# GateLoop attention and a PReLU MLP in one kernel: all steps in a new order

## The chip, the cores and the metric

The kernel runs on one core of a Trainium2 chip, and the metric is the device time of one execution in microseconds. A core has TensorE (PE, matmuls, with weight loads listed apart as PEld), VectorE (DVE), ScalarE (ACT), GpSimd (POOL) and SyncE (SP). Each runs its own instructions strictly in the order in which the program holds them; semaphores tie the engines together. Here SP does nothing but issue the 700 transfers.

## The reference

An attention block with complex gates (GateLoop) gives `attn_out`; its heads are joined and go through an MLP with a PReLU whose slope differs per feature.

```python
# q, k, v, a_re, a_im: (4, 8, 768, 48) float32
mag = np.sqrt(a_re * a_re + a_im * a_im)
scale = np.minimum(mag, 0.999) / (mag + 1e-06)
a_re_n, a_im_n = (a_re * scale, a_im * scale)
for t in range(S):
    ar, ai = (a_re_n[:, :, t, :, None], a_im_n[:, :, t, :, None])
    new_re = ar * S_re - ai * S_im
    new_im = ar * S_im + ai * S_re
    kv = np.einsum('bhd,bhe->bhde', k[:, :, t], v[:, :, t])
    S_re, S_im = (new_re + kv, new_im)
    y[:, :, t] = np.einsum('bhd,bhde->bhe', q[:, :, t], S_re)
x = attn_out.transpose(0, 2, 1, 3).reshape(B * S, H * D)   # 3072 x 384
h = x @ w_in                                               # w_in 384 x 2048
g = np.maximum(h, 0.0) + alpha * np.minimum(h, 0.0)
return (g @ w_out).astype(np.float32)                      # w_out 2048 x 384
```

## The kernel before

The recurrence is cut into 24 units (`unit`, from L563): 4 batch entries times 6 stretches of 128 tokens, with all 8 heads together. Inside a unit the tokens meet in six levels of doubling distance (1, 2, 4, 8, 16, 32, two levels per visit). For each level `meet` issues 16 small matmuls of keys with queries (L596) into `ps_lv`, ScalarE copies operands apart (WQ L660, W L676), VectorE multiplies queries and keys on by the decays (KQ L637) and masks the products (A L620, or ScalarE at L610). Then TensorE turns the keys (`ps_kt`, L708), multiplies them with the values (`ps_kv`, L720), VectorE carries the state `St` on (L728, L731), and TensorE sums the unit's result in `ps_y`: from the state (L746, 16 matmuls, two halves of 8) and from the masked products with the values VL (L760, 48 matmuls, in four steps of 12). ScalarE copies the result out (L771), SP writes it to DRAM (`ysc`).

Ahead of the units, nine tasks `gates` make decays (`decs`) and rotations (`phs`) of stretches of tokens out of `a_re` and `a_im`, mostly on VectorE and ScalarE; the results go through DRAM and come back as T and PP. `loads`, `half_rows` and `loads_v` issue the transfers of queries, keys, rotations, decays and values. `pieces` and two `weights` tasks load the MLP's weights as pairs of words and join them to f32 (L443, L445).

The MLP works on blocks of 256 tokens. `loads_x` loads a block as xT once both of its units have written their results. For the first two blocks `features` makes one feature row block at a time (TensorE L817, ScalarE L824, VectorE L826), and `outputs` sums over the features (L867). For the other ten, `two_features` makes two at a time (TensorE L839, ScalarE L848 and L852, VectorE L854), and `seven` takes the product with `w_out` apart into seven products of halves (L957, in `product`, folded by VectorE at L963 in `fold` or copied by ScalarE at L973). `all_mlp` is one task: the order inside the MLP is fixed, only what stands between its steps is not.

Every task is a Python generator that gives control back before each step; a step is one vector or scalar instruction, one transfer, or a group of matmuls. `Plan.run` goes through the string `ORDER` and advances the task of each letter by one step:

```python
    def run(self, order):
        for c in order:
            next(self.tasks[self.LETTERS.index(c)], None)
```

The letters are A to I for the nine `gates`, J `loads`, K `half_rows`, L `loads_v`, M `pieces`, N and O the two `weights`, P to Z and a to m the units 0 to 23, n `loads_x`, o `all_mlp`. Since a step issues its instruction at once, `ORDER` fixes the order of the instructions on all five engines and so also the order of the transfers in SP's queue, and with them which waits stand where. Buffers have fixed numbers of copies (three KQ, two T, one V and VL, one PP, two xT, two `ps_h`, two `ps_lv`, one each of `ps_y`, `ps_o`, `misc`), whatever the order is. The arguments of the steps (`PE(0.28, ..., n=16)`) have no effect in this program: `step` returns None.

Of the kernel before, what the change touches and what calls it, by code (L numbers as in the profile page):

```python
# [27 lines left out]


ORDER = (  # L30
    "ABMABAAABABAAAAAAABMAAAAAMAAAABABBBJMMNMAAAJABBAAKAAAKJJAAAAAAAABBBABJABBBBBBNMBNPBBBPNPJBJKJKJBJBBB"
    "PNBBBPBBBBBBBBBPPPOOOOJLJCPJJLLKKCPOJLLLMLLLLLLLMLLJJOPOPOPNOPPPPONNPPQCPPPQNQCCCCPPPPPPPPPPQQPQPCNC"
    "CCPPPPPPPPPCQQNCCCCCONCCCQOQCNPCPQQQOJMMJPPLMLLJCNQQNORCJLnLCMLLJJJLCCCLLLLQCQRCRQQCCOQNQQQoooooooLL"
    "LNQQRRQNooQQCCCCCNCooQoOoQRQoCQORCCNRRoNooooooORoQOMJONQQoooooRNNOOQQQQRQQROQOQDQQJLRLLnLJJORoLLoooo"
    "LLDMLRNNoLLLLLLooooJDooDDRoooSoSoRRRRRRRRooooooooDRRoRRoRooooRNNNRDSDoDRoDRDSOooooooooRoDoDRSSRJJJJR"
    "RSNSSRRRRDoooooDSDTOooODSLRRoSSoLMLLMJLJLLLLLooSoDSoOTSNoooooSNoOooSSoSoSNSSSSoSDooToSoSooSTSNoooOOo"
    "oNMLLLLLTTSoTSTDSOoTTSDoooooDoDSOKTNoNNNOSSSTSSTSJJJMJLSDDoooooSoooooDJLSSLoOToNTToooToOoOOoooooTTOT"
    "TToTDDTToooooUTnTTooLLLJJLJLDLLLUooooTDToDDoooLLLoLKDoJJJToTTUooDDoDDDTDJTDDDoooooUoTTUTUTTUUUUoVooo"
    "oooooUoTUUVUTTTTVooooooooUUUEJJLLLJJELLLLLLLLLJoLLooooVoEooooUUoUUUEoEVooooooEoEoUVUoUUUoooooUooooEU"
    "UVVUUVUVVVEEEooooooooVoUoKEUVKVUUUUJKKEUUUUKJJJVEVVooVooooEoooEEooEooVVVooooVVVVVVoWoWooooooVoVooJLL"  # L40
    "LJnWooVooVWoLLLLVWWEVEVEEEWEVWWLLLLLLLLEVWWVJEJoKJoooooooooooVVVWVWVVVELKVVLLLLJLJJLLLJJWoWWEWoooooo"
    "oooXXooEEEoEEoooooooooooooooooWWWWWWWoooWXoEWLLLoEoooooooooooWWooooWWoooXoXWWEEEWEEWoJLLLJoooWXWWWEW"
    "XWWWXYWXLWWLLFYXJLnLJJLoooooooXooooooooooooooXXXXXXoooooFoooooooXXFXXoXXXoXooooooooXoXoXYYooooLLLLLL"
    "LLooXXYYXooXYXYYLYooooXooooXFYFooooooXXXXYXYXFYoFYXXXLXLJLJJJLJLLLFooooooooYYoJooooooooooFoooooYYYFF"
    "YooYYooYYoJJLLLJLLJLoZoYooZooYooooFFoooFoYooYYFZoooFFLLooooooooooZooooZZYZYZYFZZYFYFYoooFZYYYZYZYYFo"
    "YooFFYooooooooooFFLLYJJJLooZooooooZZoooooooooooLnFLLFLJLLLJFooLJLLLLZaaFooooooZZoooZFaoFFZZoooooooaF"
    "FoZZZoZFFFoooooooZoooZooaaoooZoZoZZaaZFFFooFJJaoaaZooooooooooooZZZaZZZaZZaoooooooZaoaooabooooooooooo"
    "oooaaooabbZLLZLGJJLLJLJLLGLLLLLaaaoaaooaGooaoooooooJoboaoooaGoobGabaaaJJabbaLKKKoGbGoooooooooooobbbo"
    "ooGGooooGGooooboooooooooababaaGbaGGbGabaLaooooooooocoobLLJJGnKLoooooooooLoLLooobbooocbLLLLLJbbGGGoob"
    "ocooooooLLLKboboboooGGoboooocboooooobbccboocbGbGooooooocccGGoobboooobbbbooooooooooooGcGGKJGGGobcbcbo"  # L50
    "ocbJLJbbLLLJJLocccoooooooooooGooooccGcccocccGdGcoooooooooooocococoocooccoooGGGGcJLLLLLLLLLLdGcocGcoo"
    "oooooodoodooocccddcJJJcdcooooooooooooooooddLLccLHLcJJJLLLJLLdoLdHLLnoooooooodKLLLdddoddooooooooooooo"
    "ooddodddddooHeddoooeodooooodedoHdoooooooooooededdddeeoHddHooooooooeHeeoooHoooddoooooooooooooooddoeee"
    "oddoKJJJJddLLLJeJLLLJJJJLLLeoeoooooooooeHooooHooooooooooffHHooooeeeLJJLLLLLooooooHHHHHHHfooeeooeeeeo"
    "oooooeeoooooooooeoeoooeeeoeHHHfoHeHgefeoooooeeefeHeeKHooofofeeoJJHffoooooooonofHLJLLLLLLLHHooooooooo"
    "offfgoLLJLJJJLLLoofffooooooogHoLooooffoofHHfooooHHHoooooooooofffffoofoofoogoHooooHooooffooooofHHfffH"
    "ffHohhogooooooffgffgffofofhfgogooooooooooooooooggIJJLLLLLLLLJJJIJJgLLLLLLggIgoggIooooooIooooooooooog"
    "goghgIoggogoghIoogooooooogooIoogoogoghhgIhgghIhgoIooohhoooooooooioooooooohogIoIoghggghghhgIggLLLLJJn"
    "hhoooooooooooiLLLLLJLLLLLLJJooohhIhIhhIoooohhhIIihooooooooihoooooooooooooiIhooooooooooooooooooohhJoo"
    "oiiiihhohihIIIohihoooooooJhhihhihihLoohIIiooooooooooiihooooooooooooooiioihILLLoooIiiiijJJLLLJJLLLJji"  # L60
    "iJLLLLLIoiooiooiIiooioiIjiioIIIIIoIooooooooooIIIoiIoooooojiijijiijJIojjjjoooooooooooooooooooijjjjiio"
    "oiijJnJJJLLLLJLLojooooooooooooooooojjjjjjjkkjooooooooojjooojookooooooojoojoookookjkoooookkoooooooooo"
    "oojJJLLLLLLLLLjjoooooookoooooooooojookoooooookooojjjjkjkjjjkLjjkooooooooolkkoLLJJJJJooooookkkokkkook"
    "kooookokkooooolloookooklkllkkkkkloooollooooooooooolJLLLLLLLLLLJLLooooooooooloooooooooklkklkkkklkkLLL"
    "LLnlllooLLLJJLLooooooooooooooollolllloolllooooooolooolmmolloLLLLLoooooloooololmmlooooooooooolooooooo"
    "olmlmlmomomooooooooomoooooooooomoooolmlmlmooooomLLLLLLmomoooooooooLLLLoooooommoooommllmmmmmllLLLLooo"
    "oommoooooomooomooommmmmmmmmomooooooooooommmoooooooooooonoooooooooooooooooooooooooooooooooooooooooooo"
    "oooooooooooooooooooooooooooooooooooooooooooooooooooooooooooooooooooooooooooooooooooooooooooooooooooo"
    "oooooooooooooooooooooooooooooooooooooooooooooooooooooooooooooooooooooooooooooooooooooooooooooooo")

# [1072 lines left out]
```

## Time and profile before

| what | value |
|---|---|
| time of 3 runs, median (lowest to highest) | 764.36 us (761.99 to 765.21) |
| span of the profiled execution | 763.4 us |
| granted TensorE clock, mean | 0.998 |
| TensorE idle before its first matmul | 26.0 us |
| first matmul of the MLP | 84.4 us |
| last group of the last unit's product with VL (L760) | 688.8 us |
| DMA | 130.61 MB, mean 171 GB/s |

The profile is of one execution. Its page has the busy time of each engine, the span in 40 equal slices with a digit of busy tenths for each, the DMA queues, the chain of work that ended last and the costliest groups of instructions. Further views list instructions in order of time, merged where equal ones follow each other (start, time to the end of the last, engine, line, tiles and shapes, count), and busy times in stretches of the span. A matmul's time in these lists reaches from its start to the modelled end of its pipeline, so rows overlap; what TensorE really spends is read from start to start. An f32 matmul of the program stands as two passes in the trace (a transpose, L708, as one), so 16 matmuls of the program are 32 there.

Of the chain that ended last, 53% of the span lies on TensorE, 16% in transfers, 11% on VectorE and 4% on ScalarE. In the slices of VectorE and of the granted clock,

```profile
DVE  7889889998999799898986898888996765742323
PEclk9999999999999999999999999999999999999999
```

VectorE is busy through the first three quarters and TensorE's clock shows no tenth below 9.

### The profile page before, as it was taken

To read this page: it belongs to the slowest core of one execution; us is meant where nothing else is said; L and a number is where in the kernel's file an instruction comes from. 1 tells how busy PE (TensorE), PEld (TensorE's weight loads), DVE (VectorE), ACT (ScalarE), POOL (GpSimd) and SP (SyncE) were. 2 spreads that over 40 slices of the span, in tenths; PEclk is the share of its full clock that TensorE was granted. 3 is DMA by queue.
4 is the path that set the end of the run, shared out by engine and by line. 5 is a ranking of instruction groups with operands and counts; after the bars stand their busy time and mean duration, and the time that the engine had idled before them with its cause. 6 is when DMAs were issued, how large, how long until landed. Compare 5 with 4: busy or idle time off the path is not lost.

```text
span 763.4 us, 26774 instructions
## 1 busy us (share of the span) xinstructions
PE 674.9 (88%) x11728; PEld 581.2 (76%) x11728; DVE 605.4 (79%) x798; ACT 487.6 (64%) x886; POOL 13.1 (2%) x48
## 2 busy tenths in 40 slices
PE   0024578999999999999999999999999999999998
PEld 0024456776767888888888889888888988889987
DVE  7889889998999799898986898888996765742323
ACT  8868888985658576946693666756584544453330
POOL 5000000000000000000000000000000000000000
PEclk9999999999999999999999999999999999999999
DMA  9999989979677936787668854865745743421000
GB/s 257 273 258 230 267 236 274 232 216 245 192 194 201 254 83 140 210 223 187 177 170 210 234 123 102 227 188 135 185 129 171 183 104 81 112 43 53 1 21 21
DMA packets 177180, 130.61 MB, mean 171 GB/s; under 512 B 66280, under 2 KB 168424, under 8 KB 176616
## 3 DMA queue, kind: packets, MB, share of 16 engines
q1 hardware_dynamic: 177064, 128.91, 64.3%
q8 instruction: 92, 1.51, 0.9%
q14 instruction: 24, 0.20, 0.1%
HBM read 100.52 MB, written 35.42 MB: 178 GB/s over the span
## 4 chain that ended last, share of the span: by engine, by line
PE 53%; DMA 16%; DVE 11%; SPq 6%; ACT 4%; issue 2%; DVEq 0%; ACTq 0%
PE ps_h L839 19%; PE ps_o L957 17%; PE ps_lv L596 4%; PE ps_y L760 3%; DVE KQ L637 3%; DMA PP<-phs 3%; PE ps_o L867 3%; DMA T<-decs 2%; PE ps_kv L720 2%; SPq L547 2%; PE ps_y L746 2%; DMA xT<-ysc 2%; DMA shared<-in_w_out_dram 2%; DMA VL<-vsc 2%; PE ps_h L817 1%
## 5 line engine op out<-in xcount | busy, mean ns | idle before, releaser
L839 PE MATMUL ps_h<-xT,w_in_sb 128*128 128x256 f32 x960 | 228.6, 384 | 0.7 <-DVE shared L854 0.6
L839 PEld LDWEIGHTS ps_h<-xT,w_in_sb 128*128 128x128 f32 x960 | 176.9, 190 | 22.6 <-DVE shared L854 0.8
L637 DVE TENSOR_TENSOR KQ<-KQ,T 96x1024 f32<-96x1024 f32 x120 | 145.8, 1215 | 28.6 <-PE ps_lv L596 18.9
L957 PE MATMUL ps_o<-w_out_sb,shared 128*128 128x192 f32 x624 | 111.4, 329 | 0.8 <-ACT top L973 0.4
L854 DVE TENSOR_TENSOR shared<-shared,ps_h 128x512 f32<-128x512 f32 x80 | 54.5, 682 | 68.2 <-ACT shared L852 67.9
L957 PEld LDWEIGHTS ps_o<-w_out_sb,shared 128*128 128x128 f32 x624 | 102.4, 190 | 3.5 <-DVE top L963 0.8
L848 ACT ACTIVATE shared<-ps_h 128x512 f32<-128x512 f32 x80 | 47.7, 596 | 80.6 <-PE ps_h L839 80.2
L957 PE MATMUL ps_o<-shared 128*128 128x192 f32 x448 | 80.3, 331 | 0.7 <-DVE top L963 0.7
L852 ACT ACTIVATE shared<-shared,al 128x256 f32<-128x256 f32 x160 | 74.5, 505 | 1.9
L957 PEld LDWEIGHTS ps_o<-shared 128*128 128x128 f32 x448 | 72.7, 190 | 3.3 <-DVE top L963 1.4
L660 ACT COPY WQ<-KQ 96x1024 f32<-96x1024 f32 x48 | 49.9, 1039 | 33.9 <-DVE KQ L637 33.7
L596 PE MATMUL ps_lv<-WQ 96*32 96x32 f32 x2304 | 34.4, 203 | 38.2 <-DVE WQ L579 26.0
L596 PEld LDWEIGHTS ps_lv<-WQ 96*32 96x32 f32 x2304 | 26.2, 116 | 52.4 <-DVE WQ L579 26.0
L817 PE MATMUL ps_h<-xT,w_in_sb 128*128 128x256 f32 (+1 forms) x240 | 53.3, 357 | 4.5 <-DMA xT<-ysc 4.5
L867 PE MATMUL ps_o<-w_out_sb,shared 128*128 128x384 f32 x128 | 51.3, 509 | 5.6 <-DVE shared L826 4.2
L817 PEld LDWEIGHTS ps_h<-xT,w_in_sb 128*128 128x128 f32 x240 | 41.9, 203 | 16.4 <-DMA xT<-ysc 5.2
L760 PE MATMUL ps_y<-A,VL 64*48 64x64 f32 x2304 | 49.1, 225 | 4.5 <-DMA VL<-vsc 4.4
L610 ACT ACTIVATE A<-ps_lv,columns 128x64 f32<-128x64 f32 x144 | 38.3, 334 | 21.4 <-PE ps_lv L596 21.0
L771 ACT COPY T<-ps_y 48x512 f32<-48x512 f32 x48 | 27.7, 576 | 34.5 <-PE ps_y L760 33.7
L676 ACT COPY W<-KQ 96x512 f32<-96x512 f32 x48 | 30.6, 637 | 29.5 <-DVE KQ L637 29.5
L760 PEld LDWEIGHTS ps_y<-A,VL 64*48 64x48 f32 x2304 | 39.4, 123 | 11.0 <-DMA VL<-vsc 5.8
L596 PE MATMUL ps_lv<-KQ,W 96*32 96x32 f32 x1536 | 23.4, 203 | 15.9 <-ACT W L676 15.8
(108 smaller groups left out, 955.8 us busy)
## 6 DMA issues: line engine op xcount, KB each, us to landing
T<-decs SPq DMA_DIRECT2D x48, 384.0 KB
PP<-phs SPq DMA_DIRECT2D x24, 387.0 KB
KQ<-in_q_dram SPq DMA_DIRECT2D x48, 192.0 KB
phs<-gate SPq DMA_DIRECT2D x14, 577.5 KB
decs<-gate SPq DMA_DIRECT2D x7, 1152.0 KB
KQ<-in_k_dram SPq DMA_DIRECT2D x40, 192.0 KB
vsc<-in_v_dram SPq DMA_DIRECT2D x24, 288.0 KB
VL<-vsc SPq DMA_DIRECT2D x48, 144.0 KB
```

Source lines behind the costliest of these rows:

```text
L596: nc.tensor.matmul(t[64 * i + j:64 * i + j + HC // 2, p], lhsT=keys(n, g), rhs=queries(n, g), start=True, stop=True)
L610: nc.scalar.activation(a[:, :, cols], t[:, :, at:at + name], AF.Copy, scale=s)
L637: nc.vector.tensor_tensor(out=x, in0=x if x0 is None else x0, in1=m, op=ALU.mult)
L660: nc.scalar.copy(z.rearrange("p i n t -> p i (n t)").rearrange("p i (m h) -> p m i h", h=h), bass.AP(tensor=KQ.tensor, offset=KQ.offset + ...
L760: nc.tensor.matmul(o, lhsT=Vp[h][64 * i:64 * i + 64, s, e_ * D:(e_ + 1) * D], rhs=a, start=False, stop=(s == 1 and h == LEVELS[-1]))
L817: nc.tensor.matmul(p, lhsT=w_in_sb[:, f // 2, kk, f % 2 * P:(f % 2 + 1) * P], rhs=x_of[m][:, kk, c * P:(c + n) * P], start=(kk == 0), stop ...
L839: nc.tensor.matmul(p[:, i], lhsT=w_in_sb[:, f // 2, kk, i * P:(i + 1) * P], rhs=x_of[m][:, kk], start=(kk == 0), stop=(kk == NK - 1))
L848: nc.scalar.activation(gt, p, AF.Relu, scale=-1.0)
L852: nc.scalar.activation(some_, some_, AF.Copy, scale=al_1[:, f + i:f + i + 1])
L854: nc.vector.tensor_tensor(out=gt, in0=gt, in1=p, op=ALU.add)
L867: nc.tensor.matmul(sums[0], lhsT=gt, rhs=w_out_sb[:, f], start=(f == start), stop=(f == stop))
L957: nc.tensor.matmul(z, lhsT=a[:, i], rhs=w[:, i], start=i == 0, stop=i == F2 - 1)
```

## The change

The string `ORDER` is another one, of the same length and with every letter as often as before. Nothing else differs. Each engine's instructions are the same in kind, shape and number; which of them stand next to each other changes, and so does the number of separate semaphore waits. The first and the last lines of the diff, and one out of its middle:

```diff
 ORDER = (
-    "ABMABAAABABAAAAAAABMAAAAAMAAAABABBBJMMNMAAAJABBAAKAAAKJJAAAAAAAABBBABJABBBBBBNMBNPBBBPNPJBJKJKJBJBBB"
+    "AAAAAABBBABJAAAAAKAAAAABAAABMAAAAAABBMMMMJJMBBKABAAAAAAAAAAAMAAAAJBBBBBBBBBBNNBBJPPPJJJNJBBJPKLBBBBB"
...
-    "oooaaooabbZLLZLGJJLLJLJLLGLLLLLaaaoaaooaGooaoooooooJoboaoooaGoobGabaaaJJabbaLKKKoGbGoooooooooooobbbo"
+    "oooZaGaooooooooooabbabLGoaooGaLZZLLLaaaaaoGoooooooaoJLoaooooLLJoGGboooLKaooooLJLoooaabaaJbbGGGbboGba"
...
-    "oommoooooomooomooommmmmmmmomooooooooooommmoooooooooooonoooooooooooooooooooooooooooooooooooooooooooo"
+    "LLLLLLmmommoooomoooooooooooooomomommmlmmnooooooooooooooooooooooooooooooooooooooooooooooooooooooooooo"
     "oooooooooooooooooooooooooooooooooooooooooooooooooooooooooooooooooooooooooooooooooooooooooooooooooooo"
```

On TensorE the four steps of L760 of a unit now often stand with a single matmul of L839 or L957 between them, where they stood in a row or next to L596, for example, in the order of the changed program's TensorE rows:

```
L760 Matmult ps_y<-A,VL (12 matmuls)
L839 Matmult ps_h<-xT,w_in_sb 128x256
L760 Matmult ps_y<-A,VL (12 matmuls)
L839 Matmult ps_h<-xT,w_in_sb 128x256
L760 Matmult ps_y<-A,VL (12 matmuls)
L839 Matmult ps_h<-xT,w_in_sb 128x256
L760 Matmult ps_y<-A,VL (12 matmuls)
```

More of the change, by code (lines that the diff above doesn't have):

```diff
@@ L30 @@
 ORDER = (
-    "ABMABAAABABAAAAAAABMAAAAAMAAAABABBBJMMNMAAAJABBAAKAAAKJJAAAAAAAABBBABJABBBBBBNMBNPBBBPNPJBJKJKJBJBBB"
[L32 to L45, printed above, removed]
@@ L46 @@
-    "YooFFYooooooooooFFLLYJJJLooZooooooZZoooooooooooLnFLLFLJLLLJFooLJLLLLZaaFooooooZZoooZFaoFFZZoooooooaF"
-    "FoZZZoZFFFoooooooZoooZooaaoooZoZoZZaaZFFFooFJJaoaaZooooooooooooZZZaZZZaZZaoooooooZaoaooabooooooooooo"
-    "oooaaooabbZLLZLGJJLLJLJLLGLLLLLaaaoaaooaGooaoooooooJoboaoooaGoobGabaaaJJabbaLKKKoGbGoooooooooooobbbo"
-    "ooGGooooGGooooboooooooooababaaGbaGGbGabaLaooooooooocoobLLJJGnKLoooooooooLoLLooobbooocbLLLLLJbbGGGoob"
-    "ocooooooLLLKboboboooGGoboooocboooooobbccboocbGbGooooooocccGGoobboooobbbbooooooooooooGcGGKJGGGobcbcbo"
@@ L51 @@
[L51 to L65, printed above, removed]
@@ L66 @@
-    "olmlmlmomomooooooooomoooooooooomoooolmlmlmooooomLLLLLLmomoooooooooLLLLoooooommoooommllmmmmmllLLLLooo"
-    "oommoooooomooomooommmmmmmmmomooooooooooommmoooooooooooonoooooooooooooooooooooooooooooooooooooooooooo"
+    "AAAAAABBBABJAAAAAKAAAAABAAABMAAAAAABBMMMMJJMBBKABAAAAAAAAAAAMAAAAJBBBBBBBBBBNNBBJPPPJJJNJBBJPKLBBBBB"
+    "BKNBNPLLOBBBBBBBBBBNPJJOCJJPPONPLLLOOLPPPPPPOOOOPOPPLKPCCCCNNCKMLLMPPPQLLLLLQQQCQQCPPPPPPPPPPPCQCPPP"
+    "PQCCCCCCCCQQNNJJNQPPPPPPPPQCMJJOOOQJQPPCCCCQNQQQQLMLROJOJLLLLnRNCCCCCCCCLLQoooRQCCNLQQQNQoRRQQQooooM"
@@ new lines @@
+    "oLLLLORCCCCQQCooCLLMQRCQROOOoooQOCRNRNQRNNNNQQQQQRJJQJJRNRooDoQQQQQJLLNLRNRLnoooooooooooooRoJDRJOOOO"
+    "DORoRRRoDooooooooJLooLoSDSDooDRRRRRMoooooooRLDDooRoRRRooooLDoooooooDSoooLoRRoDDDSoooooooooooDSSoNNNS"
+    "LMJLLLLRRRLSNSMSDJJOooooooooooORRROROoNSRSSRJLLRRSSMODSSDLLLLoooooooooooDooSNNNoSNSSSSJLTTNooooooSSS"
+    "SSooooSSSSJTooSLOOOTOLMTTSODTTNSNLLLLLLDoSDNTJSSSSSSNTSMKJJooooooooJOSSNOooLToToDJOOOooTnTDDooooLDLL"
+    "ooDTLJLLJLLTDTDLooooooDTTTToTToooTTTLLooUUoUTTDooooooTLDTooTTTDDDDDDLDDoooooDUTTTTLUUTJToJJJJTDUoToT"
@@ new lines @@
+    "TTTUULLUoVooooooooooVLVLLUUUJUJLoooooooooLUUUoooooooVUUUUUUUUoooUVEoLLEoEUUooUoLVVVVUEUUUVVEVLooooLL"
+    "LKEUVUKoEEUVUoJJJJJUVUVLUUUULooooVooVVooooKoEWoooVVooKVVVVVEEooLoLJJLoVoooLKLVVoVWLLLooLoEEooVoooVVV"
+    "WEoWWWoooooVWVLLVWVVWLLooooVWJEJJJJnoWWVoWVoEWoVEEEEEEEVLVVVLLLWWEEWEJJooooooXoooEJEoooooooooooooooo"
+    "ooJLLLLLLLXEELJWWWWEEWLLLEEoooooJooooooooWoooooooooWWWWoXWoooooooWoooWEWWWEEJXXXXWEEXoooEXXWWWooXooW"
+    "EoWooooWXXWWWLXWWFLYXXXJYoooooooooooooooooooXXXXoXooooJooYLLLXXXXooXXoooooooXoooXXXXLYXYYnYLoooYXXXo"
@@ new lines @@
+    "LLFYYoLLLLLLJFoooooooooooooooooFXoXoXYYYYJoFFJJXXXXXKJLFYYYoooooooooooooooooYYYoYooYFFZYFYLoooLLLYYY"
+    "YJLoooooooooooooooooooLLLLYFFZooFYYFoJJYJFZYoooooJLLLLooYoooooFYLZYFYFZZZooFFFFFYoYoYoJYYKJKKKYYYKZZ"
+    "ZLJooooooooooooooLLJFFoooLLLoLoooooJJFZZZaooaZnFFoFFoZZZFoooooooooooooFLaLLLLLooooooooooooaZaZaoZFFo"
+    "oFJJJoLooooFaZZZZZZZZFoFFFFLFKooooooooooooooooooZoooooZoooZZZZooooooooaaaZZZboaooooooZoZoZaaaZZKGGaG"
+    "oooZaGaooooooooooabbabLGoaooGaLZZLLLaaaaaoGoooooooaoJLoaooooLLJoGGboooLKaooooLJLoooaabaaJbbGGGbboGba"
@@ new lines @@
+    "aooooobGbGooooooLLLKaoooaoJabKbaGJJcLooLLoLaaaaLGLLLLoobbcoonobbJJJJJooooLooGooooooooooooooLbJbbbGGG"
+    "bGGoooooobbbbbboooooooooooooooooooocGobboooobbbccccGLLLLGGGcbbbbcGGooocoooooooooboboooobccccbcooooob"
+    "bbboGccooooLLoJoooLoJJooooooLLLLLLGGGJccccccGGGGGLGdoooooooooooooooocccoccooooLoLGddoLooocoocJoooooo"
+    "oocdddcccdccddcoooodoooooodLLcoooHocddcoooccJJJHcccdHeooooooooLoddHHdHeJooooooooooooooooddLdddoodddo"
+    "oooJHHHHLnLooodddoooooooooooooooooooLJdoooLLLedooooddLddeeeeeeeddLdooooooeoLKLLHoooooooHLLodHeedeodo"
@@ new lines @@
+    "oooooodeJLeddeooodooHooooooJJoeeeooHHeeeHHHdeeeooooooooooooooeeLJLLLJHoooooHHoooeHoooeeoooeooooeeeJo"
+    "oooLLLLLLLoooJJfLLLHoJooooeeJffHHHHHHHHHHHHHHHfoooooooooHHeoJoeffeoeeeeeLooooooHffffooooofnooooooooo"
+    "oooooooooooofffgfffIooJooooooooooooooooJLffffffLLfoofooooooooffLgLgoLIIofoooLLJJIoooooooooooooofooff"
+    "gffoIIgLLLLLfggfgoogoffLJJJoofofooooofggggffoLhIIfggIgLLooooLfLooooogooooofoooooooooooooogLhggggggoo"
+    "ooooooooggIogooogoghJLLJhohoIgLLLLgggLohhhhggoooooLgoJooJghhIhhhghghJJJhLLggggLLLinhooLLoLooooIJoooo"
@@ new lines @@
+    "oJJoohIIooohIhIooohhhIhihIILLLoooooIooIhoooohohhooooooohooooohooooooooLLoLohhhihhooooooooihoohiIiiii"
+    "IioLhiooooohJoJJoohohhhhhILiiiLoooooooooJLoooooiiLoioLLoooooooooooooooJJiiiiiLLLLLLjjooIioJooooooooi"
+    "iiiioooLiooLILiiijiojjJIJjjIiiJiiooooooooIjjooiJoijooooooiIIIIIIIIjjjjIIiiiiiIjjjoonoooooooooooooooo"
+    "ojjoojjojjjLLJkLLLjookjooooooooooooooooooooooooooooooooooojjooJooJoJjkjooooLojkLjjkkkkkjkjjjoooLLLLL"
+    "LLLookooooooojooojojkkjjjLjjLJkkkoookooooooooooooooooooooLLkJLkkooooooooooooooooookkkLkkJJJJJJLLLLLk"
@@ L68 @@
+    "kkLlooooookkoollloooooooooookkklllllkkkkLJLoLoooooloooJklooookoookllkllkloooooooLkkkLooooonllollooll"
+    "ollmmJJooooooooooooolllooooloooooooooooLooooomLoloolooooooolllmmmllLlmmmmlooomoLLLooLLLLLLooooooooLo"
+    "loooooolooolmooomlomooooooooooooooollmmmmmmommmmoooooooooooooooomoooooooooommmlooooooomomoLLLLLomLLL"
+    "LLLLLLmmommoooomoooooooooooooomomommmlmmnooooooooooooooooooooooooooooooooooooooooooooooooooooooooooo"
     "oooooooooooooooooooooooooooooooooooooooooooooooooooooooooooooooooooooooooooooooooooooooooooooooooooo"
```

## The prediction

> **What bounds the kernel now.** First the page's busy times and its row of instruction packets, then stretches of the span, then TensorE's own lines in order of time.
>
> ```profile
> span 763.4 us, 26774 instructions
> PE 674.9 (88%) x11728; PEld 581.2 (76%) x11728; DVE 605.4 (79%) x798; ACT 487.6 (64%) x886; POOL 13.1 (2%) x48
> q8 instruction: 92, 1.51, 0.9%
> ...
> 133.00:154.00 21.00, 20.21 (x446) 15.28 (x446) 21.00 (x28) 19.93 (x37) 0.88 (x1) 1.00 0.93 228
> ...
> 154.00:302.00 148.00, 143.98 (x2596) 114.51 (x2595) 133.81 (x171) 99.00 (x186) 0.36 (x4) 1.00 0.75 195
> 302.00:690.00 388.00, 385.10 (x6890) 341.95 (x6890) 312.43 (x395) 239.61 (x461) 0.95 (x10) 1.00 0.61 157
> ```
>
> The last three rows give a stretch, its length, then the busy time of TensorE (PE), its weight loads, VectorE (DVE), ScalarE (ACT) and POOL, the granted clock, the DMA share and GB/s. VectorE has no idle time from 133 to 154 us and 10% from 154 to 302; TensorE's idle share falls from 3% there to under 1% from 302 to 690. So VectorE sets the pace up to about 300 us, and TensorE after that: behind that point every nanosecond of TensorE time counts, and work of another engine counts only where TensorE waits for it.
>
> What TensorE's time consists of is read from starts: the time from one row's start to the next row's.
>
> ```profile
> 226.02 0.46 PE L596 MATMUL ps_lv<-WQ 96*32 96x32 f32 x32
> 226.41 0.55 PE L760 MATMUL ps_y<-A,VL 64*48 64x64 f32 x24
> 226.89 0.46 PE L596 MATMUL ps_lv<-KQ,W 96*32 96x32 f32 x32
> 227.28 0.55 PE L760 MATMUL ps_y<-A,VL 64*48 64x64 f32 x24
> 227.76 2.86 PE L839 MATMUL ps_h<-xT,w_in_sb 128*128 128x256 f32 x12
> 230.46 1.78 PE L867 MATMUL ps_o<-w_out_sb,shared 128*128 128x384 f32 x5
> ...
> 620.66 1.89 PE L839 MATMUL ps_h<-xT,w_in_sb 128*128 128x256 f32 x8
> 622.48 0.46 PE L596 MATMUL ps_lv<-WQ 96*32 96x32 f32 x32
> 622.75 0.49 PE L596 MATMUL ps_lv<-KQ 96*32 96x32 f32 x32
> 623.17 1.57 PE L957 MATMUL ps_o<-shared 128*128 128x192 f32 x8
> ...
> 688.83 1.59 PE L760 MATMUL ps_y<-A,VL 64*48 64x64 f32 x96
> 690.35 0.92 PE L957 MATMUL ps_o<-shared 128*128 128x192 f32 x4
> 691.10 2.75 PE L839 MATMUL ps_h<-xT,w_in_sb 128*128 128x256 f32 x12
> 693.69 2.77 PE L957 MATMUL ps_o<-w_out_sb,shared 128*128 128x192 f32 x16
> ```
>
> I call the attention's matmuls (L596, L708, L720, L746, L760) small and the others big. Twelve passes of L839 between big neighbours take 693.69 - 691.10 = 2.59 us; right behind small ones they take 230.46 - 227.76 = 2.70, so **entering big from small costs 0.10**. Eight passes ahead of a small group take 622.48 - 620.66 = 1.82 against 8 x 0.216 = 1.73: **leaving big for small costs 0.09**. A group of 32 L596 alone takes 0.39 and two in a row take 623.17 - 622.48 = 0.69: each start of an L596 run costs 0.09. 96 passes of L760 in a row take 690.35 - 688.83 = 1.52; four groups of 24 take 4 x 0.48 = 1.92: each start of an L760 run costs 0.13. Likewise L746: 8 matmuls 0.58, 16 in a row 1.03, so 0.14 a start. L708 shows no such cost (four take 0.33 in any place).
>
> **The change, part by part.** Every engine's instructions are the same in number and shape (PE 5960 matmuls, DVE 798, ACT 886, SP 700 transfers); only the order moves, so the sum consists of what order costs.
>
> *TensorE's runs.* Counted in the two orders, old to new: the product with V (L760) often stands in pieces of 12 matmuls with a single big matmul between pieces, where it stood in pieces of 24 to 96 passes next to other small work. Entries from big into small other than L708 go from 77 to 124: +47 x 0.09 = +4.2 us. Entries from such small work into big, 81 to 124: +43 x 0.10 = +4.3. Starts of L760 runs, 55 to 85: +30 x 0.13 = +3.9. Starts of L596 runs, 93 to 74: -19 x 0.09 = -1.7. Starts of L746 runs, 35 to 24: -11 x 0.14 = -1.5. Sum **+9.2 us**. A lone big matmul between two small groups hardly occurs in the trace; if it costs only half of an entry and an exit, the sum falls by about 60 x 0.1 = 6, which I keep as the low end (+3.2).
>
> *Semaphore instructions.* TensorE's separate waits go from 223 to 236. One takes 51 ns in the trace on its sequencer (PEldq, L596 and L760): 0 where queued matmuls cover it, 13 x 0.051 = 0.7 where none do. I take 0.3, since a start behind such a wait usually shows no gap. VectorE gets 23 more and ScalarE 7; on the stretch where VectorE paces that is at most 1 us, within the bounds below.
>
> *What stands ahead of TensorE on VectorE.* By the mean duration of each row I sum the VectorE work that must be over before TensorE can have done so much of its own. For 60 us of TensorE work: 147.5 us before, 137.2 now; for 70: 157.3 and 156.1; for 100: 185.2 and 185.7; for 150: 240.9 and 234.3; for 200: 291.6 and 287.4; for 250: 338.6 and 337.6. TensorE passed its 200 us mark at 302.3, just behind the VectorE work that it needed (301.4), so there the lead of the new order is worth **-4.2**; bounds 0 (TensorE paces already) and -6.6 (the row at 150).
>
> *Transfers.* SP's queue is put together anew with all its waits. The bytes ahead of the same TensorE mark are at most 3.4 MB fewer (26.5 for 29.9 at 40 us) and at most 1.5 MB more (101.5 for 100.0 at 400 us). In the ramp DMA is 93 to 95% busy, but the last needed transfer was issued 5 to 15 us before TensorE used it, so I take 0. At the 400 us mark the new order's last transfer stands where the old one issued at 503.5, and TensorE was there at 507.2: with the 3 to 6 us that L551 and L797 take to land this could cost 0 to 2. The cover is TensorE's other work; it is thinnest there. POOL's few fills (13.1 us in all) move with their units: 0.
>
> *Packets of instructions.* The change counts the arrival of TensorE's instruction packets (92 of 16 KB, a packet per 256 instructions). In the trace TensorE starts that come over 0.33 us late stand at an instruction with a wait, 52 to 57 ns behind the end of the VectorE or ScalarE work it waits for or at a landing; none is left for a packet, even where 256 instructions hold under 2 us of work. So spreading the bursts brings 0 here, and its price is the runs above.
>
> *The clock.* The granted clock is 0.51 from 129.5 to 133.0 us and 1.00 in every later stretch; ten L817 and L867 starts in it are late by 1.6 us in all. The new order can lose or gain one such stretch: -1.6 to +1.6, taken as 0, as VectorE paces there. [...]
>
> *Sum:* 763.4 + 9.2 + 0.3 - 4.2 = 768.7 us of span. The median of the runs, 764.36, lies 1.0 above the profiled span: **769.7, rounded to 770 us.**
>
> **The rivals.** About 0.5% (3.8 us) is what a measurement here tells from no change, so "same" reaches from 760.5 to 768.2.
>
> *A, TensorE's waits vanish (faster).* After 150 us TensorE's late starts at waits sum to 12.0 us (the largest: 1.4 us at 181 us and 1.1 at 214, L867 for L826 or L890; 0.9 at 457, L957 for L963). If the new order covers all of them, 770 - 12 = 758. For it: TensorE waits whose own work covers the VectorE or ScalarE chain by less than 0.5 us fall from 7 to 3. Against it: those with under 2 us rise from 33 to 50. It decides faster once 9.2 of the 12.0 us are gone.
>
> *B, the runs cost half (same).* If the lone big matmuls pay half, the sum is 764.4 + 3.2 + 0.3 - 4.2 = 764. For it: weight loads that are fetched early would hide part of the entry. Against it: each of the 80-odd entries in the trace pays, whatever stands around it.
>
> *C, TensorE paces all along and waits more (much slower).* No lead, and the 17 more thin covers cost 0.27 us each, as the old ones did (33 with some 9 us): 764.4 + 9.5 + 4.6 = 778.5. For it: TensorE is already 97% busy from 154 to 302. Against it: VectorE's 21.00 of 21.00 us just before.
>
> *That the change does what it says*, that is, that packets are late now, would give a gain; no start shows one, and I hold it inside A.
>
> **How the numbers follow.** Forecast (766 to 774) 0.44, A 0.20, B 0.22, C 0.14. Slower than by 0.5% holds the forecast and C: 0.58; same is B: 0.22; faster is A: 0.20. The range reaches down into A, where all but 2.3 us of the waits would have to go (760), and up to C with part of its price (779). The likeliest case's own range is 766 to 774.
>
> **What would show it.** Right: the last L760 group, at 688.83 now, starts near 698 (13 us more TensorE work stands before it, less the lead), and only some 65 us of TensorE work is left behind it; the group of unit 9 at 304.46 starts within 3 us of that; L760 groups of 24 passes between L839 or L957 rows take 0.48 plus 0.19. Wrong: if such a lone L839 matmul takes 0.43 with no surcharge (B), if TensorE's listed waits after 150 us fall under 3 us (A), or if its idle share from 302 us on rises above 1% (C). Late starts without a releaser in the new trace would refute the reading of the packets.

## The result and the profile after

| | before | the new order |
|---|---|---|
| time, median (lowest to highest) | 767.36 us (761.99 to 770.82, 10 runs; the first three 764.36) | 773.87 us (771.86 to 777.03, 10 runs) |
| ratio to before, 95% interval | | 1.0092 [1.0063, 1.012] |
| span of the profiled execution | 763.4 us | 773.2 us |
| granted clock, mean | 0.998 | 0.980 |

The new order is slower by about 0.9%, and 773.87 us lies within 4 us of the forecast of 770, just inside its range of 766 to 774. By the medians the difference is 6.5 us; between the two profiled executions, which the tables below compare, it is 9.8, since that of before took 765.21 us, 2.2 less than its median, and that of the new order 774.99, 1.1 more. The page after, with the rows that answer to those shown of before: busy times, the row of instruction packets, and the three stretches (length, then busy time of PE, PEld, DVE, ACT and POOL, granted clock, DMA share, GB/s).

```profile
span 773.2 us, 26818 instructions
...
PE 683.2 (88%) x11728; PEld 583.3 (75%) x11728; DVE 608.3 (79%) x798; ACT 491.8 (64%) x886; POOL 12.2 (2%) x48
...
q8 instruction: 92, 1.51, 0.8%
...
133.00:154.00 21.00, 18.27 (x402) 13.10 (x401) 20.46 (x28) 19.15 (x34) 0.33 (x1) 1.00 0.92 245
154.00:302.00 148.00, 142.10 (x2590) 111.53 (x2592) 130.48 (x164) 97.33 (x182) 0.36 (x4) 0.98 0.72 194
302.00:690.00 388.00, 382.66 (x6712) 337.57 (x6703) 314.69 (x393) 242.06 (x458) 0.95 (x10) 1.00 0.60 158
```

From 302 to 690 us TensorE does fewer matmul passes (6712, before 6890) in almost the same busy time (382.66, before 385.10). The missing passes are nearly all small ones, and the work done there is some 5 us less for 2.4 us less of busy time, so the rest costs some 3 us more. Its idle share there is 1.4%, and the clock of the middle stretch fell to 0.98. The group of the product with V in both pages, before first (columns: busy us, mean ns, idle us ahead of it and what ended most of that):

```profile
L760 PE MATMUL ps_y<-A,VL 64*48 64x64 f32 x2304 | 49.1, 225 | 4.5 <-DMA VL<-vsc 4.4
```

```profile
L760 PE MATMUL ps_y<-A,VL 64*48 64x64 f32 x2304 | 55.4, 227 | 9.1 <-issue 8.9
```

Before, what it waited for was a transfer. Now it is "issue": nothing that the profile shows.

**Where the time went.** I follow one quantity through both traces: how much TensorE work without any switch cost has been done. "Switches" is the prediction's price list applied to the starts passed so far; "rest" is the time less work and switches (the ramp, waits, half clock).

| work done | time before / new | switches before / new | rest before / new |
|---|---|---|---|
| 40 us | 136.6 / 129.2 | 3.8 / 3.8 | 92.7 / 85.1 |
| 130 us | 238.6 / 235.3 | 9.6 / 12.1 | 99.0 / 92.9 |
| 150 us | 260.9 / 264.6 | 10.8 / 14.0 | 99.9 / 100.2 |
| 300 us | 425.7 / 434.9 | 20.5 / 26.3 | 104.8 / 108.3 |
| 609 us (all) | 758.2 / 768.0 | 36.1 / 46.2 | 113.0 / 112.7 |

At the end the rest is the same in both (113.0 and 112.7), and the difference of 9.8 us is, in size, the switches' 10.1. But the new order had gained 6 to 8 us of rest up to 130 us of work, and lost it all before 150, that is between 235 and 265 us. TensorE there, in order of time (start, time to the modelled end of the last, line, tiles, count, idle time ahead and releaser):

```profile
250.51 0.49 PE L596 MATMUL ps_lv<-KQ,W 96*32 96x32 f32 x32
250.93 0.32 PE L760 MATMUL ps_y<-A,VL 64*48 64x64 f32 x4
254.60 0.88 PE L760 MATMUL ps_y<-A,VL 64*48 64x64 f32 x20 [3.36 <-issue]
255.41 5.00 PE L957 MATMUL ps_o<-w_out_sb,shared 128*128 128x192 f32 x16
260.25 2.11 PE L839 MATMUL ps_h<-xT,w_in_sb 128*128 128x256 f32 x9
```

The wait stands between two passes of one step, where the program has no wait, and the 16 passes of L957 behind it take 5.0 us, where 16 behind small ones at 696.13 us take 2.9: the granted clock is 0.51 from 252.9 to 259.8. I call such a stretch half clock. Counting TensorE's instructions, all nine such waits after 150 us stand 62 to 65 instructions ahead of a multiple of 256 (at 172, 246, 251, 271, 305, 345, 393, 421 and 534 us). The trace lists 92 transfers of 16 KB in the queue of instruction packets (q8) for TensorE's 23456 passes and weight loads and 236 separate waits, so some 256 instructions to a packet, and in all nine TensorE goes on 1.3 to 1.6 us after one of these transfers has landed: the fetch that the trace lists as number 27 ran from 252.30 to 253.23, and TensorE restarted at 254.60. I therefore take these points, and not the multiples of 256 themselves, for the packets' bounds. (Why they stand some 62 ahead of those multiples isn't shown.) These waits sum to 11.7 us, the half clock behind the two longest (251 and 421 us) to 3.6. In the other direction, TensorE's late starts at waits for engines and transfers after 150 us (starts over 0.13 us later than the work and the switch ahead of them account for) fell from 10.8 to 3.2 us.

### The profile page after: what moved, and what is told of

Its sections match the earlier page's. It is cut to its first block, busy times and chain, and to the rows that moved or that the text cites. A ratio compares the mean times of both kernels' runs of the same rounds, so it can differ in the third digit from the quotient of the medians.

```text
span 773.2 us, 26818 instructions
## 1 busy us (share of the span) xinstructions
PE 683.2 (88%) x11728; PEld 583.3 (75%) x11728; DVE 608.3 (79%) x798; ACT 491.8 (64%) x886; POOL 12.2 (2%) x48
## 4 chain that ended last, share of the span: by engine, by line
PE 79%; DVE 7%; ACT 7%; DMA 4%; issue 2%; SPq 1%; DVEq 0%
PE ps_h L839 28%; PE ps_o L957 24%; PE ps_y L760 5%; PE ps_lv L596 5%; PE ps_o L867 4%; PE ps_h L817 3%; PE ps_kv L720 3%; PE ps_y L746 3%; PE ps_kt L708 2%; DVE KQ L637 1%; DMA decs<-gate 1%; PE ps_h L957 1%; DMA shared<-in_w_in_dram 1%; DMA vsc<-in_v_dram 1%; DMA gate<-in_a_re_dram 1%
## 5 line engine op out<-in xcount | busy, mean ns | idle before, releaser
L839 PE MATMUL ps_h<-xT,w_in_sb 128*128 128x256 f32 x960 | 230.4, 384 | 0.7 <-issue 0.7
L839 PEld LDWEIGHTS ps_h<-xT,w_in_sb 128*128 128x128 f32 x960 | 176.5, 190 | 23.4 <-issue 1.1
L957 PE MATMUL ps_o<-w_out_sb,shared 128*128 128x192 f32 x624 | 115.7, 334 | 0.4 <-ACT top L973 0.4
L957 PEld LDWEIGHTS ps_o<-w_out_sb,shared 128*128 128x128 f32 x624 | 104.3, 193 | 3.6 <-ACT top L973 0.7
L957 PE MATMUL ps_o<-shared 128*128 128x192 f32 x448 | 85.8, 337 | 0.0
L957 PEld LDWEIGHTS ps_o<-shared 128*128 128x128 f32 x448 | 73.7, 192 | 3.2 <-DVE top L984 0.2
L596 PE MATMUL ps_lv<-WQ 96*32 96x32 f32 x2304 | 34.2, 203 | 46.3 <-DVE WQ L579 33.6
L596 PEld LDWEIGHTS ps_lv<-WQ 96*32 96x32 f32 x2304 | 26.2, 116 | 58.9 <-DVE WQ L579 29.4
L760 PE MATMUL ps_y<-A,VL 64*48 64x64 f32 x2304 | 55.4, 227 | 9.1 <-issue 8.9
L760 PEld LDWEIGHTS ps_y<-A,VL 64*48 64x48 f32 x2304 | 41.7, 123 | 27.9 <-issue 25.2
L610 ACT ACTIVATE A<-ps_lv,columns 128x64 f32<-128x64 f32 x144 | 36.7, 330 | 10.5 <-PE ps_lv L596 10.2
L596 PE MATMUL ps_lv<-KQ,W 96*32 96x32 f32 x1536 | 24.4, 203 | 17.1 <-ACT W L676 16.3
```

The source lines that it names most:

```text
L596: nc.tensor.matmul(t[64 * i + j:64 * i + j + HC // 2, p], lhsT=keys(n, g), rhs=queries(n, g), start=True, stop=True)
L610: nc.scalar.activation(a[:, :, cols], t[:, :, at:at + name], AF.Copy, scale=s)
L760: nc.tensor.matmul(o, lhsT=Vp[h][64 * i:64 * i + 64, s, e_ * D:(e_ + 1) * D], rhs=a, start=False, stop=(s == 1 and h == LEVELS[-1]))
L839: nc.tensor.matmul(p[:, i], lhsT=w_in_sb[:, f // 2, kk, i * P:(i + 1) * P], rhs=x_of[m][:, kk], start=(kk == 0), stop=(kk == NK - 1))
L957: nc.tensor.matmul(z, lhsT=a[:, i], rhs=w[:, i], start=i == 0, stop=i == F2 - 1)
```

## The experiments

Each ratio is to runs of before on the same chip (medians of before 767.8 to 769.5 us). Where an edit moves letters of `ORDER`, one or two of its lines are shown.

### Do the packets' bounds matter at all? e1, e5, e2

```diff
+        idle = ps.tile([P, DM], F32, tag="o", name="ps_o")
+        for i in range(32):
+            nc.tensor.matmul(idle[0:32, 0:32], lhsT=ident[0:32, 0:32], rhs=ident[0:32, 0:32], start=True, stop=True)
         plan.run(ORDER)
```

32 tiny matmuls are 128 TensorE instructions: every later instruction moves by half a packet (e1 in the old order, e2 in the new one). In e5 the loop runs to 64 in the old order, a whole packet, so the bounds fall where they were.

> The order before, with 32 tiny matmuls of the identity (128 instructions) put ahead of TensorE's first matmul, where TensorE stands idle for 26 us. They cost nothing themselves; they only move every packet boundary of TensorE's stream by half a packet. Theory P (packets bound: the next packet of 256 instructions is asked for only when TensorE enters the one before, so a packet that holds less than about 4 us of work is left before the next is there, and the orders are laid out around their boundaries): after 150 us of the span the packets with under 4 us of work go from 1 to 19, and what they lack sums to 34 us, so 25 to 40 us slower, as waits that no engine releases. Rival S (only switches between small and big matmuls and waits for other engines count; the waits without a releaser in the new order are chance): within 2 us of before.

> The order before with 64 tiny matmuls ahead (256 instructions, one whole packet), the control of the half packet: every boundary stands where it stood. P: within 2 us of before, no waits without a releaser after 150 us. If the added instructions themselves cost, or the longer stream does, it is slower like the half packet was (+36 us).

> The new order with the same 128 instructions ahead. P: packets with under 4 us go from 11 to 15, and their lack from 4 to 19 us (by 4.4 us: 9 to 25), so 12 to 18 us slower than the new order, about 20 to 28 above before. S: as the new order, 7 us above before. If the waits for packets in the new order are chance, they appear at other places with the same sum, and the time is that of the new order.

Measured: e1 803.69 us, 1.0475 [1.0417, 1.0532]; e5 765.74, 0.997 [0.9942, 0.9998]; e2 785.14, 1.0254 [1.019, 1.0318], some 11 us above the new order (12 to 18 were expected), with waits for packets at other steps. The list of TensorE's waits of e1 (us in total, times, longest):

```profile
PE ps_lv L596 <- issue: 15.2, 7, 4.6
...
PE ps_y L760 <- issue: 12.5, 7, 3.9
...
PE ps_y L746 <- issue: 2.0, 1, 2.0
```

Waits without a releaser, half clock included, cost 37.5 us after 150 us in e1 and none in before; the time grew by 36. Same order, same work, twice as much padding: no loss. So the old order too is laid out around the packets' bounds, and its trace shows no wait for a packet because of that. That settles the prediction's zero for the packets as an error of reasoning: it had looked at 256 instructions anywhere, and what counts is the work between two bounds, set against the moment of the fetch (e9 and e11 below).

### Do the switches set the end? e3, e4, e6

e3 puts the four L760 steps of each unit in a row in the new order, e4 moves them together in the old order, e6 moves some of them apart there. Two lines of e3:

```diff
-    "LMJLLLLRRRLSNSMSDJJOooooooooooORRROROoNSRSSRJLLRRSSMODSSDLLLLoooooooooooDooSNNNoSNSSSSJLTTNooooooSSS"
+    "LMJLLLLRRRLSNSMSDJJOooooooooooORRRROOoNSRSSRJLLRRSSMODSSDLLLLoooooooooooDooSNNNoSNSSSSJLTTNooooooSSS"
```

> The new order with the four L760 steps of each unit in a row, each moved ahead to the first; the big matmuls between them follow. Switches alone (S): starts of L760 runs go from 85 to 24 and the switch cost by the prices of the prediction from 46.2 to 31.9 us, so 14 us faster than the new order, 6 to 7 below before. Packets alone: packets with under 4 us from 11 to 13, their lack from 4 to 13 us, so 9 us slower than the new order. Both (P): about 5 us faster than the new order, within 3 us of before, with more waits without a releaser than in the new order (about 12 us there) and a larger share of big matmuls in a row.

> The order before with L760 steps of a unit moved together only where no packet gets shorter than the shortest of before (3.9 us): starts of L760 runs go from 55 to 27, of L596 runs from 93 to 80, the switch cost from 36.1 to 30.9 us. Both theories: 4 to 6 us faster than before. If switches cost nothing where TensorE is full (the lone big matmul hides them), the same as before.

> The order before with some L760 steps moved apart by big matmuls where no packet gets shorter than 3.9 us: entries from big into small other than L708 go from 77 to 93, starts of L760 runs from 55 to 64, the switch cost from 36.1 to 40.5 us. If TensorE's own time sets the end (the sum of the prediction): 4 us slower. If TensorE has slack against the chain through VectorE and ScalarE, as the regrouped order suggests, where 5.2 us saved on switches came back as 7.8 us of waits: 0 to 2 us slower, with waits shorter by as much as the switches cost.

| | time, us | ratio to before | switches | rest |
|---|---|---|---|---|
| e3 | 768.56 | 1.001 [0.9974, 1.0046] | 46.2 to 31.9 | 112.7 to 119.1 |
| e4 | 767.92 | 0.9997 [0.9962, 1.0033] | 36.1 to 30.9 | 113.0 to 120.8 |
| e6 | 772.00 | 1.0056 [1.0024, 1.0087] | 36.1 to 40.5 | 113.0 to 115.9 |

e6 adds 4.4 us of switches and is 4.3 us slower (0.56% of 768). That agrees with switches paid in full, but the interval reaches from 1.8 to 6.7 us, so half the price isn't excluded by the time alone. The rests are those of single executions, and that of before was 2 to 3 us faster than the medians of before, so a part of each rest above 113.0 is that. Taken away the switches aren't gained in full. e4 is a miss: 5.2 us of switches went and the time stayed. The line of TensorE's longest list of waits that changed, in before and then in e4:

```profile
PE ps_lv L596 <- ACT W L676: 15.8, 6, 7.4
```

```profile
PE ps_lv L596 <- ACT W L676: 20.3, 11, 7.4
```

Five more starts of L596 wait for ScalarE's copy W. The pieces of L760 that stood between two L596 groups had covered that copy; gathered in a row they no longer do. In e3 the gain of 14.3 us is cut to some 5 by a new packet wait of 3.3 us at 297 us with half clock behind it, and by 3 us more of waits for engines.

### Was the loss at 251 us a chance of one execution? e8

> The new order once more, for its waits. P: waits without a releaser stand at the same packets as in the first profile (the longest at packet 29, 251 us) with about the same sum (12 us after 150 us, without the clock). Chance: other packets, another sum.

The new order again: 778.66 us, 1.0126 [1.0084, 1.0167]. Its trace has a wait of 3.76 us at the same instruction (7362 of TensorE's stream), 2.15 us at the same one as at 421 us, and five smaller ones at places of the first trace; of the nine the smallest are missing, and two or three small ones are new.

### Do longer packets help? e7, e9, e10

e7 moves 82 TensorE steps of the new order so that the packets holding under 4.0 us of work fall from 11 to 4; the 4.0 is an estimate: in the new order's trace the middle fetch starts 1.4 us after TensorE has come to the bound before and takes 1.0, and TensorE goes on some 1.4 after it has landed, 3.8 together. e9 changes two spots alone, e10 four more:

```diff
-    "EoWooooWXXWWWLXWWFLYXXXJYoooooooooooooooooooXXXXoXooooJooYLLLXXXXooXXoooooooXoooXXXXLYXYYnYLoooYXXXo"
+    "EoWooooWWWWLWWFLYJYoooooXXXXXXooooooooooooooXXXXoXooooJooYLLLXXXXooXXoooooooXoooXXXXLYXYYnYLoooYXXXo"
...
-    "oocdddcccdccddcoooodoooooodLLcoooHocddcoooccJJJHcccdHeooooooooLoddHHdHeJooooooooooooooooddLdddoodddo"
+    "oocdddcccdccddcoooodoooooodLLcoooHoddoooJJJHdHoocococcccceooooLoddHHdHeJooooooooooooooooddLdddoodddo"
```

> The new order with 82 of the units' TensorE steps moved past a few steps of the MLP or of other engines, so that packets after 150 us with less than 4.0 us of work fall from 11 to 4 and what packets lack to 4.4 us from 8.6 to 3.6 us; the switch cost stays (46.0 for 46.2). P: waits without a releaser and the half clock behind them, some 15 us in the new order, fall to 4 to 8; moved steps cost 1 to 4 us of new waits for other engines; 4 to 9 us faster than the new order, so within 4 us of before. If these waits don't set the end (S): as the new order.

> The new order with two spots changed and no other: at 251 us one L596 pair of a unit and the two VectorE and two ScalarE steps behind it move behind three L957 products, so the packet that held 3.5 us of TensorE work holds 4.7; at 421 us three pieces of the product with V (L760) move in between L957 products, so the packet that held 3.4 us holds 4.5. Switches cost 0.4 us more. Theory P (a short packet alone makes the wait, and the half clock behind it follows from the wait): the waits of 3.5 and 2.2 us at these spots go and with them the half clock at 253 and 424 us, together 5.7 + 3.6 - 0.4 = about 9 us; since some of it comes back as waits for VectorE or ScalarE (7 of 10 us did when 82 steps were moved), 4 to 9 us faster than the new order, 765 to 770. Rival M (where the packets are late is decided by the traffic on the chip, and the wait comes back at a neighbouring packet): within 2 us of the new order, waits without a releaser of 10 us or more in all after 150 us, at other places.

> The same two spots, and four more moves of single L760 pieces (at about 173, 217, 244 and 531 us) that lengthen the packets there: packets under 4.0 us lack 1.0 us in all after 150 us, where the new order lacks 4.0. Switches cost as much as in the new order. P: the waits at 172.5, 246.3 and 534.1 us (1.0 + 0.9 + 1.0) go as well: 1 to 3 us faster than with the two spots alone, 763 to 768. Rival M: as the new order, within 2 us, with as much waiting without a releaser. Rival W (the pieces that moved away had covered VectorE's and ScalarE's chains): the waits for packets go, waits for engines grow by the same, and the time is as with the two spots alone or more.

All three miss. e7: 781.24 us, 1.0153 [1.0116, 1.019]; waits for engines after 150 us rose from 3.2 to some 10.9 us, those without a releaser fell only from 15.3 to 11.9 (half clock included). e9: 773.23, 1.0056 [1.0027, 1.0084]; e10: 775.89, 1.0111 [1.0057, 1.0166]; neither can be told from the new order. Rival M's number, within 2 us of the new order with 10 us of packet waits or more, fits both: these waits sum to 10.9 us in e9 and 10.5 in e10, though most of them stand at the old instructions. In e10 waits for engines grew too, as rival W has it; the longest, 2.9 us at 534 us, is for the copy W. The spot at 251 us in e9:

```profile
254.88 0.27 PE L596 MATMUL ps_lv<-KQ,W 96*32 96x32 f32 x6
256.98 0.55 PE L596 MATMUL ps_lv<-KQ,W 96*32 96x32 f32 x26 [1.83 <-issue]
```

The packet now holds 4.7 us of TensorE work instead of 3.5, and the wait is 2.0 us instead of 3.5, still at the same instruction number. At 421 us it holds 4.5 instead of 3.4, and the wait is 2.35 us, not less than before. So a short packet is only one half of it; the theory that it makes the wait by itself falls. The other half is when the fetch runs.

### Is it the fetch that is late? e11, e12

TensorE's packet 27 is fetched 5.0 us after TensorE had come to the bound before, where it had waited until 247.31 us; I count each fetch from that point. The middle one of all fetches from 150 to 690 us has 1.4 (before: 1.2, the longest 4.7). That a fetch is asked for at that point isn't shown: some fetches of the new order start up to 1.3 us before TensorE's matmuls come to it. SP's queue in the new order's trace just then:

```profile
247.06 0.38 SPq L361 DMA_DIRECT2D decs<-gate  x1
247.53 0.44 SPq L523 DMA_DIRECT2D V<-in_v_dram  x1
256.13 0.97 SPq L776 DMA_DIRECT2D ysc<-T  x2
257.20 0.42 SPq L263 DMA_DIRECT2D gate<-in_a_re_dram  x1
257.67 0.55 SPq L525 DMA_DIRECT2D V<-in_v_dram  x1
```

The store of the decays, 1152 KB, goes out 0.25 us ahead of that point (247.31). e11 moves this one transfer behind the unit's two result stores, e12 also the gate load that was issued at 415.60 us, ahead of the late fetch at 421. No instruction of another engine moves.

```diff
-    "EoWooooWXXWWWLXWWFLYXXXJYoooooooooooooooooooXXXXoXooooJooYLLLXXXXooXXoooooooXoooXXXXLYXYYnYLoooYXXXo"
+    "oWooooWXXWWWLXWWEFLYXXXJYoooooooooooooooooooXXXXoXooooJooYLLLXXXXooXXoooooooXoooXXXXLYXYYnYLoooYXXXo"
...
-    "oocdddcccdccddcoooodoooooodLLcoooHocddcoooccJJJHcccdHeooooooooLoddHHdHeJooooooooooooooooddLdddoodddo"
+    "oocdddcccdccddcoooodoooooodLLcoooHocddcoooccJJJcccHdHeooooooooLoddHHdHeJooooooooooooooooddLdddoodddo"
```

> The new order with one step of SP's queue moved and nothing on any other engine: the store decs<-gate (L361, 1152 KB) that is issued at 247.06 us, just ahead of the request for TensorE's packet 27, moves behind the two ysc stores of the unit that ends then, some 4 us later. TensorE's instructions, the packets' bounds and the work in each are those of the new order. Theory T (a packet's fetch waits behind the bulk transfer that was issued just ahead of it; the stall is a late fetch that meets a packet without enough work): packet 27 is fetched within 2 us of its request, the wait of 3.5 us at 251 us and the half clock behind it go, 3 to 6 us faster than the new order: 768 to 771. Theory P (the short packet alone makes the wait): the packet is as short as before, so the wait stays, within 2 us of the new order, 772 to 776.

> The same, and the second gate load of the group at 415.60 us (L263, in_a_im, 576 KB) also moves behind the two ysc stores of its unit, some 7 us later, out of the traffic that was ahead of packet 50's fetch (requested at 417.4, fetched at 420.55). T: the wait of 2.2 us at 421 us shrinks to under 1 us, and the half clock at 424 us goes: 1 to 4 us faster than with the one transfer, 765 to 770; the gate load's own landing comes ahead of its first reader on VectorE. P: both waits stay, 772 to 776.

The spot at 251 us in e11, with TensorE's instructions as in the new order:

```profile
252.21 0.32 PE L760 MATMUL ps_y<-A,VL 64*48 64x64 f32 x4
253.14 0.54 PE L760 MATMUL ps_y<-A,VL 64*48 64x64 f32 x20 [0.62 <-issue]
253.61 2.87 PE L957 MATMUL ps_o<-w_out_sb,shared 128*128 128x192 f32 x16
```

The busy tenths of the DMA engines in slices of 0.2 us from 246 to 254 us, in the new order and then in e11:

```profile
DMA  0000000002999999999999989989950300000000
```

```profile
DMA  9994243100000000000000030000000000000000
```

The digit 3 is the fetch. In the new order it comes as soon as the traffic of the store and of the load of V behind it (168 KB) has ended (252.3 us); in e11 it comes at 250.6 with nothing else under way.

The fetch ran 2.05 us behind its point instead of 5.0, the wait shrank from 3.5 us to 0.74, and the clock stayed whole (16 passes of L957 in 2.87 us). The other two executions agree: 5.4 us late in e8, 2.1 in e12. So some 3 us were that traffic's, and 2 us of delay remain without any ahead. At 150 us of work done e11's rest is 96.2 us, 4.0 less than the new order's. In e12 the late fetch at 421 us runs 1.8 us behind its point instead of 3.1, and the wait shrinks from 2.17 to 0.79 us with no half clock behind it; in e11, where the gate load had not moved, these were 3.5 and 2.40, without half clock as well. The wait in the new order and then in e12:

```profile
423.18 0.55 PE L760 MATMUL ps_y<-A,VL 64*48 64x64 f32 x24 [2.10 <-issue]
```

```profile
426.86 0.55 PE L760 MATMUL ps_y<-A,VL 64*48 64x64 f32 x24 [0.72 <-issue]
```

**That a late fetch behind a bulk transfer makes the longer part of these two waits is shown at both spots.** For the other seven waits it isn't shown.

The end is another matter: e11 777.63 us, 1.0118 [1.0081, 1.0156], e12 775.02, 1.0089 [1.0057, 1.012], no gain. What took it back first, in e11, SP's queue and then TensorE:

```profile
256.00 0.39 SPq L361 DMA_DIRECT2D decs<-gate  x1
260.55 0.39 SPq L263 DMA_DIRECT2D gate<-in_a_re_dram  x1
260.99 0.49 SPq L525 DMA_DIRECT2D V<-in_v_dram  x1
```

```profile
265.79 0.31 PE L720 MATMUL ps_kv<-V,T 64*64 64x48 f32 x2
268.01 1.14 PE L720 MATMUL ps_kv<-V,T 64*64 64x48 f32 x62 [1.91 <-DMA V<-in_v_dram]
```

The store came 9 us later, not the 4 I had reckoned, since it stands behind stores that wait for the unit's end. The gate load behind it waits for its buffer, and the load of V behind that went out at 260.99 instead of 257.67. TensorE waited 2.0 us for V, and the clock was halved for 6.8 us afterwards. By 175 us of work nothing of the 4.0 us was left. Later on e11 has a wait of 2.6 us at 532 us that the new order doesn't have.

No order that I ran beats before by more than its interval allows but for e5, whose order is before's own.

## Why the prediction was right, and where it wasn't

**The switches: right.** Forecast +9.2 us from counts and prices read in the trace before; +10.1 in the table, 9.8 in the span. A lone L839 matmul between two L760 groups was the doubtful case (rival B: it pays half). The last unit in the new trace:

```profile
700.23 0.58 PE L760 MATMUL ps_y<-A,VL 64*48 64x64 f32 x24
700.73 0.70 PE L839 MATMUL ps_h<-xT,w_in_sb 128*128 128x256 f32 x2
701.36 0.55 PE L760 MATMUL ps_y<-A,VL 64*48 64x64 f32 x24
701.84 0.70 PE L839 MATMUL ps_h<-xT,w_in_sb 128*128 128x256 f32 x2
702.47 0.55 PE L760 MATMUL ps_y<-A,VL 64*48 64x64 f32 x24
```

From start to start the lone matmul takes 701.36 - 700.73 = 0.63 us, 0.43 for its two passes and 0.20 for going in and out; the group takes 0.48 behind it. These are the 0.48 and 0.19 of the prediction, so B falls; e6 agrees with the price in the time of a whole kernel, within its interval.

**The packets: wrong, "spreading the bursts brings 0".** The step that failed is the inference from "no start is late for a packet" to "packets cost nothing here". The missing waits were the result of the old order's layout: after 150 us each of its packets but one holds 4 us of TensorE work or more, in the new order eleven hold less. This is seen only with the bounds where the waits stand; cut at the multiples of 256, 13 stretches of before and 12 of the new order hold less than 4 us. e1 shows what the same instructions cost with the bounds half a packet further on. The sign that I had set for this (late starts without a releaser) came, and it refutes the reading.

**VectorE's lead: right in kind, not kept.** Forecast -4.2 us at 302 us of span. That VectorE sets the pace up to there didn't follow from the prediction's own rows, which have TensorE 97% busy from 154 us on; the lead came from the ramp. The new order was 7.4 us ahead at 40 us of work and 4.0 at 110; the wait for packet 27 with its half clock cost 5.5 us at 251 us and put it behind.

**The clock: forecast 0 within 1.6, measured a loss of 3.6 us** behind the two longest packet waits. The half clock that the trace before had was in the ramp (3.4 us). The new order has 20.5 us of it there (72.0 to 92.5), which makes most of the mean clock's fall to 0.980; what it cost is inside the ramp's rest and isn't told apart.

**TensorE's waits (rival A): its premise came true, its result didn't.** The late starts at waits fell from 10.8 (12.0 by the prediction's count) to 3.2 us, a gain of 7.6 that my sum had not counted; the sign, under 3 us, was reached or nearly, as the list of TensorE's waits has 7.3 and 2.4. Together: +10.1 switches, +11.7 packets, +3.6 clock, -7.6 waits after 150 us, some -4 in the ramp up to there (the rest at 150 us of time is some 94 us before and 90 in the new order) and, to make up the 9.8 of the span, -4 that no listing here places. So the forecast of the time held by luck: two errors met, packets and clock at nothing, the engines' waits at nothing as well. The luck is narrow, too: e8, the same program on another chip, took 778.66 us. **Rival C's** sign (idle share over 1% from 302 us) came too, but by packets, not by thin covers.

**The other signs.** The last L760 group starts at 702.5 us, not near 698: the 13 us more of TensorE work ahead of it came, the lead of 4.2 did not. Unit 9's group starts at 305.1 (all but its first pass at 306.3, behind a packet wait), within 3 us of 304.46, as forecast. The 13 more semaphore instructions (51 ns each) cost nothing that can be seen, nor does any landing that TensorE waits for; but the place of one store made packet 27 late, so the zero for the transfers was wrong by that way. e11 shows how thin the transfers' cover is, as 3 us of delay in one load of V cost 2.0 us of TensorE time.

**What stays open.** Of the seven orders made to gain (e3, e4, e7, e9 to e12) only e3 ended clearly below the one it started from, by 5 of the 14 us that it took out. Each trace names some of the new waits (W's copy, V's load, other packets), but which packet is late next isn't predicted by anything here: that would need the moment of each fetch in the traffic of each order.

## What to carry to other kernels

In a program with thousands of small TensorE instructions, a trace without packet waits may owe that to its layout, as that of before does (36 us in e1): shift the instructions by half a packet once and see what it costs before any reordering is priced. Look for a bulk transfer issued just ahead of a fetch whose packet holds little TensorE work (here the store of 1152 KB ahead of packet 27: 3.5 us of wait with it there, 0.74 without), and move the transfer only if nothing else in its queue is then late. A gain at one spot in a schedule this tight is worth what is left of it at the end, and that has to be run.

## What the runs showed of the hardware that I had not expected

- A shift of all TensorE instructions by 128 costs 36 us of 768 (e1), by 256 none (e5).
- From 150 to 690 us of the new order a packet's fetch of 16 KB takes 0.9 to 1.5 us (in before up to 2.0), and TensorE goes on 1.3 to 1.6 us after it has landed, in all nine waits. The waiting instruction stands 62 to 65 ahead of a multiple of 256, and in the new order the fetch starts between 1.3 us ahead of its point and 5.0 us behind it. At 251 us it started when the traffic ahead of it had ended; with the store moved away it was still 2.05 us late (e11).
- In the list of TensorE's matmul waits before (PE) none is without a releaser; with the same order and its bounds half a packet further on such waits, half clock included, cost 37.5 us after 150 us (e1).
- The granted clock halved for 3.4 us behind a wait of 2.2 us (421 us) and for 6.8 us behind one of 3.5 us (251 us), and in before for 3.4 us behind one of 2.03 us (ahead of L596 at 129.22 us, for the copy W). A wait of 2.2 us was enough here, and e11's of 0.74 wasn't.
- The length of a wait alone doesn't decide it: e11 has a wait of 2.4 us at 424 us with no half clock behind it and one of 1.6 us at 366 us with it. In the trace of the new order the stretches at half clock ahead of its end start at 72.05, 252.96 and 423.62 us and last 20.48, 6.83 and 3.41 us, that is 6, 2 and 1 times the shortest; the starts lie 180.9 and 170.7 us apart, 53 and 50 times the shortest. In the 3.41 us just ahead of the falls at 252.96 and 423.62 TensorE was busy for 1.71 and 1.31 us, 50 and 38%. Of the stretches of before from 150 to 690 us, counted in steps of 3.41 us from its own fall at 129.55, the least busy has 64% (180.75 to 184.16), and the clock stays whole behind it. These are two executions; what decides a fall beyond them isn't shown.
